# A feature-map attention with a squared-ReLU feed-forward: the last chunk's tiles of two batches each stored by one transfer

## The chip, the cores and the metric

The kernel runs on one core of a Trainium2 chip. A core has five engines with instruction queues of their own: TensorE (PE, matrix products; its weight loads are listed as PEld), VectorE (DVE), ScalarE (ACT), GpSimd (POOL) and SyncE (SP). SP does no arithmetic; here it issues transfers. ACT and POOL issue transfers too. The transfers themselves are carried by 16 DMA engines that all queues share. The metric is the device time of one execution in microseconds, lower is better.

## What is computed

Eight batches of 576 tokens with 8 heads of 64 values go through an attention with a feature map, and its output, 4608 tokens of 512 values, through two matrix products with a squared ReLU between them:

```python
def phi(x):
    proj = np.einsum('bhsd,df->bhsf', x, w_phi)
    proj = proj - np.max(np.abs(proj), axis=-1, keepdims=True)
    return np.concatenate([np.exp(proj), np.exp(-proj)], axis=-1)
q_p, k_p = (phi(q), phi(k))
kv = np.einsum('bhsf,bhsd->bhfd', k_p, v)
z = np.sum(k_p, axis=2)
num = np.einsum('bhsf,bhfd->bhsd', q_p, kv)
den = np.einsum('bhsf,bhf->bhs', q_p, z)[..., None] + 1e-06
attn = num / den                        # 8 x 8 x 576 x 64
x = attn.transpose(0, 2, 1, 3).reshape(4608, 512)
h = np.maximum(x @ w_in, 0.0)           # w_in 512 x 2048
out = h * h @ w_out                     # w_out 2048 x 512, out 4608 x 512 float32
```

## The kernel before

The feed-forward works in nine chunks of 512 tokens (`NCH = 9`). The chunks 0 to 7 hold the first 512 tokens of one batch each. The ninth, chunk 8, collects what is left: the last 64 tokens of all eight batches. It has four tiles of 128 tokens, `tt` = 0 to 3, and tile `tt` holds the tails of the batches `2*tt` (partitions 0 to 63) and `2*tt + 1` (partitions 64 to 127). In the output those two groups of 64 rows lie 576 rows apart.

For each chunk, `ffn_in` (line 745) makes the hidden layer on PE, `relu_sq` (line 721) applies ReLU and squares on ACT, DVE and POOL, and `ffn_out` (line 807) makes one tile of 128 tokens by 512 outputs per `tt` in PSUM (line 816), copies it on ACT or DVE into one of three float32 buffers `ot` (line 824), and stores it. In chunks 0 to 7 the store is one transfer of 128 rows on SP (line 835). In chunk 8 it is two transfers of 64 rows, one for each batch (line 832), both on SP except for tile 2, whose second half ACT issues.

The last tile of the program, chunk 8 and `tt` = 3, goes through `last_out` (line 772). There the 512 output columns are split into two halves of 256, with a PSUM bank each (line 780). Half 0 is copied by ACT (line 796), half 1 by DVE (line 794), into the buffer `otl`, and each half is stored by two transfers of 64 rows (line 803): batch 6 on SP, batch 7 on ACT. So half 0 and half 1 make four transfers.

All work is first recorded as operations by `add`, and then issued in the order of a table of numbers, `ORDER` (line 892); each engine runs its instructions in the order in which they are issued. `pin` ties each instruction to the one before it on its engine. An operation's instructions are those that its function `fn` issues when its turn comes. A transfer that is issued on SP or ACT waits at the head of that engine's queue until the copy it stores has been made. At the end of the program SP waits for all transfers to land, and then the engines meet and the program closes (recorded as line 1029).

Of the kernel before, what the change touches and what calls it, by code (L numbers as in the profile page):

```python
# [20 lines left out]
def act_cost(n):  # L21
    return max(n / 1200 + 0.050, 0.105), n / 1200 + 0.165 + SEM


def dve_cost(n):
    return n / 960 + 0.064, n / 960 + 0.150 + SEM
# [6 lines left out]
def pe_cost(n, each):  # L33
    return n * each, n * each + 0.165 + SEM
# [23 lines left out]
class Plan:  # L58
# [6 lines left out]
    def add(self, eng, cost, fn, r=(), w=(), opens=None, closes=None, dma=None, tiled=False, release=False, what=""):  # L65
        op = Op(eng, cost, fn, opens, closes, dma, tiled, release, len(self.ops), what)
        before = {}

        def after(o, wait):
            before[o] = max(before.get(o, 0.0), wait)  # L70

        for t in r:
            o = self.writer.get(t)
            if o is not None:
                after(o, 0.0 if o.eng == eng == "PE" else 1.0)
        for t in w:
            o = self.writer.get(t)
            if o is not None:
                after(o, 0.0 if o.eng == eng else 1.0)
            for o in self.readers.get(t, ()):  # L80
                after(o, 0.0 if o.eng == eng else 1.0)
        for t in r:
            self.readers.setdefault(t, []).append(op)
        for t in w:
            self.writer[t] = op
            self.readers[t] = []
        before.pop(op, None)
        for o, wait in before.items():
            o.succ[op] = wait
        op.n = len(before)  # L90
        self.ops.append(op)
        self.banks.extend(op.opens)
        return op
# [18 lines left out]
def kernel(  # L112
# [10 lines left out]
    nc = tc.nc  # L123

    B, H, S, D = q.shape
# [10 lines left out]
    def dep(i, before, kind):  # L136
        tc.add_manual_dep(i, before, mybir.DependencyInfo(kind, mybir.DependencyReason.DATA), reason="order")

    def pin(ins):
        i = ins.ins  # L140
        before = last_on.get(i.engine)
        if before is not None:
            dep(i, before, mybir.DependencyClass.NoSync)
        last_on[i.engine] = i.name
        if now[0].seq in GATES:
            dep(i, plan.ops[GATES[now[0].seq]].ins, mybir.DependencyClass.Sync)
        now[0].ins = i.name
        return ins
# [5 lines left out]
    def sb(name, shape, dt=BF16):  # L154
        return pool.tile([P, *shape], dt, name=name)

    def ring(name, n, shape, dt=BF16):
        return [sb(f"{name}{i}", shape, dt) for i in range(n)]
# [28 lines left out]
    ot = ring("ot", 3, [DM], F32)  # L187
    otl = sb("otl", [DM], F32)
# [4 lines left out]
    def copy(out, in_):  # L193

        if now[0].eng == "DVE":
            pin(nc.vector.tensor_copy(out=out, in_=in_))  # L196
        else:
            pin(nc.scalar.activation(out=out, in_=in_, func=ACT.Copy))
# [4 lines left out]
    def ps1(g):  # L203
        return psum[:, g.base, :]
# [564 lines left out]
    opb = {}  # L769
    oslot = [0]  # L770

    def last_out(c, tt, part):

        if part == 0:
            opb[c, tt] = [Bank(1, "op"), Bank(1, "op")]
        gs = opb[c, tt]
        def mm(half):
            def fn():
                for mc in range(4 * part, 4 * part + 4):
                    pin(nc.tensor.matmul(out=ps1(gs[half])[:, :256], lhsT=h2[c % 2][mc // 4][:, mc % 4, tt * P : (tt + 1) * P],  # L780
                                         rhs=wout[mc // 4][:, mc % 4, half * 256 : half * 256 + 256],
                                         start=(mc == 0), stop=(mc == MC - 1)))
            return fn
        for half in range(2):
            add("PE", pe_cost(4, 0.109), mm(half),
                r=[("wout", part)] + [("h2", c % 2, 4 * part + i, tt) for i in range(4)],
                w=[gs[half]], opens=gs[half] if part == 0 else None, what="F2h")
        if part < 3:
            return
        for half in range(2):  # L790
            def fn(half=half):
                o, i_ = otl[:, half * 256 : half * 256 + 256], ps1(gs[half])[:, :256]
                if half:
                    pin(nc.vector.tensor_copy(out=o, in_=i_))
                else:
                    pin(nc.scalar.activation(out=o, in_=i_, func=ACT.Copy))
            add("DVE" if half else "ACT", (dve_cost if half else act_cost)(256), fn, r=[gs[half]],
                w=[("otl", half)], closes=gs[half], what="oth")
        for half in range(2):
            for u, (name, e) in enumerate((("SP", nc.sync), ("ACT", nc.scalar))):  # L800
                def fn(half=half, u=u, e=e):
                    b = 2 * tt + u
                    pin(e.dma_start(out=out[b * S + 512 : b * S + 576, half * 256 : half * 256 + 256],
                                    in_=otl[u * 64 : u * 64 + 64, half * 256 : half * 256 + 256]))
                add(name, (0.5, 2.4), fn, r=[("otl", half)], what="stl")

    def ffn_out(c, tt, part):
        if (c, tt) == (NCH - 1, 3):
            last_out(c, tt, part)
            return  # L810
        if part == 0:
            opb[c, tt] = Bank(1, "op")
        g = opb[c, tt]
        def fn():
            for mc in range(4 * part, 4 * part + 4):
                pin(nc.tensor.matmul(out=ps1(g), lhsT=h2[c % 2][mc // 4][:, mc % 4, tt * P : (tt + 1) * P],  # L816
                                     rhs=wout[mc // 4][:, mc % 4, :], start=(mc == 0), stop=(mc == MC - 1)))
        add("PE", pe_cost(4, 0.216), fn, r=[("wout", part)] + [("h2", c % 2, 4 * part + i, tt) for i in range(4)],
            w=[g], opens=g if part == 0 else None, what="F2")
        if part == 3:  # L820
            sl = oslot[0] % 3
            oslot[0] += 1
            def fn():
                copy(ot[sl], ps1(g))
            o = add("ACT", act_cost(512), fn, r=[g], w=[("ot", sl)], closes=g, what="ot")
            plan.either((o, "DVE", dve_cost(512)))
            for u in range(2 if c == NCH - 1 else 1):
                def fn(u=u):
                    if c == NCH - 1:
                        b = 2 * tt + u  # L830
                        e = nc.scalar if tt == 2 and u else nc.sync
                        pin(e.dma_start(out=out[b * S + 512 : b * S + 576, :], in_=ot[sl][u * 64 : u * 64 + 64, :]))
                    else:
                        o = out[c * S : c * S + 512, :].rearrange("(p j) n -> j p n", j=4)[tt]
                        pin(nc.sync.dma_start(out=o, in_=ot[sl]))
                add("ACT" if c == NCH - 1 and tt == 2 and u else "SP", (0.5, 0), fn, r=[("ot", sl)], dma=(0.37 if c == NCH - 1 else 0.74, HW_IN, "st"), what="st")
# [22 lines left out]
    for c in range(NCH + 1):  # L859
        if c + 1 < B:  # L860
            b = c + 1
# [18 lines left out]
    for op in plan.arrange():  # L880
        if op.seq in FILL:
            now[0] = filler
            bank, n, col = FILL[op.seq]
# [150 lines left out]
```

## Time and profile before

| | us |
|---|---|
| median of three runs | 352.79 (352.58 to 352.99) |
| the profiled execution, whole | 352.66 |
| its span, from the first to the last instruction | 350.5 |
| PE busy | 338.9 |
| DVE busy | 273.2 |
| ACT busy | 228.4 |
| POOL busy | 96.8 |

The span is what the profile covers; the whole time of that execution is 2.2 us longer. The time of the runs is the whole time. The granted clock of PE was 1.000 over the span.

The profile is read from several views. The page gives busy times, a strip of 40 equal slices with the busy share in tenths, and the chain of waits that ended last. The same chain can be had in order of time. A view of instructions in order of time lists start and duration, with `SPq` and `ACTq` for a transfer's issue on that queue, which counts the issuing alone and not the transfer; consecutive instructions of one line are merged into one row with their count (x5). A view of the DMA packets gives, for a window, their number and bytes, by size, and for each queue the share that their durations make of 16 engines' time in the window. The queue of SP is q1 there, that of ACT is q10.

### The profile page before, as it was taken

How to read it: one execution, taken by the hardware profiler on the slowest of the kernel's cores; microseconds unless marked ns; L12 is line 12 of the kernel's file. 1: busy time of each engine (PE TensorE's matmuls, PEld its weight loads, DVE VectorE, ACT ScalarE, POOL GpSimd, SP SyncE). 2: the span in 40 equal slices, each digit the busy share in tenths (PEclk: the TensorE clock that was granted, in tenths of full speed). 3: DMA queues.
4: the chain of work that ended last, by engine and by line, in shares of the span. 5: the costliest groups of instructions: out<-in, count | busy, mean ns of one | idle time of the engine just before them, and what ended most of it. 6: DMA issues, size and time to landing. Idle time of an engine off the chain costs nothing.

```text
span 350.5 us, 8394 instructions
## 1 busy us (share of the span) xinstructions
PE 338.9 (97%) x3344; PEld 192.5 (55%) x3380; DVE 273.2 (78%) x521; ACT 228.4 (65%) x431; POOL 96.8 (28%) x144
## 2 busy tenths in 40 slices
PE   8889999999999999999999999999999999999995
PEld 5669976544654555455546554555545544444452
DVE  4999998899979988989877897999786932374332
ACT  4999897599779775787898569885954222321110
POOL 8735450397518510289104050000000000000000
PEclk9999999999999999999999999999999999999999
DMA  8999999899999997899957499792762610100114
GB/s 95 180 200 202 197 98 150 154 123 172 176 187 132 161 146 147 190 121 158 147 121 136 56 143 175 138 189 54 148 144 70 138 45 30 62 30 0 62 62 118
DMA packets 114917, 44.31 MB, mean 126 GB/s; under 512 B 83392, under 2 KB 110400, under 8 KB 114880
## 3 DMA queue, kind: packets, MB, share of 16 engines
q0 software_dynamic: 45216, 18.36, 46.7%
q1 hardware_dynamic: 69344, 25.14, 35.1%
q8 instruction: 26, 0.43, 0.5%
q10 hardware_dynamic: 320, 0.30, 0.2%
q14 instruction: 11, 0.09, 0.1%
HBM read 36.77 MB, written 9.44 MB: 132 GB/s over the span
## 4 chain that ended last, share of the span: by engine, by line
PE 78%; DVE 10%; ACT 7%; issue 3%; DMA 1%; DVEq 0%; ACTq 0%; POOLq 0%
PE psum L816 30%; PE psum L751 27%; PE psum L607 5%; PE psum L355 4%; PE psum L473 3%; PE psum L762 3%; DVE va L443 3%; ACT qf L592 2%; PE psum L577 2%; DVE mk L410 2%; DVE mq L517 2%; DVE h L735 2%; ACT kn L416 1%; PE psum L780 1%; DMA xk<-in_k_dram 1%
## 5 line engine op out<-in xcount | busy, mean ns | idle before, releaser
L816 PE MATMUL psum<-wout,h 128*128 128x512 bf16 x524 | 130.1, 379 | 2.2 <-issue 0.6
L751 PE MATMUL psum<-xT,win 128*128 128x512 bf16 x448 | 108.1, 379 | 0.3
L726 ACT ACTIVATE hr<-psum 128x512 bf16<-128x512 f32 x97 | 56.3, 596 | 68.8 <-PE psum L751 43.7
L816 PEld LDWEIGHTS <-h 128*128 128x128 bf16 x560 | 50.9, 98 | 55.4 <-issue 0.8
L751 PEld LDWEIGHTS <-win 128*128 128x128 bf16 x512 | 47.4, 98 | 54.0 <-issue 2.5
L735 DVE TENSOR_TENSOR h<-hr 128x512 bf16<-128x512 bf16 x143 | 55.9, 414 | 9.9 <-ACT hr L726 9.5
L592 ACT ACTIVATE qf<-psum 128x1024 bf16<-128x1024 f32 (+1 forms) x60 | 54.6, 942 | 10.7 <-PE psum L577 9.4
L517 DVE TENSOR_REDUCE mq<-psum 128x8 f32<-128x1024 f32 (+1 forms) x40 | 44.1, 1109 | 3.0 <-PE psum L355 2.1
L728 DVE TENSOR_SCALAR hr<-psum 128x512 bf16<-128x512 f32 x47 | 31.8, 685 | 17.7 <-PE psum L751 16.1
L410 DVE TENSOR_REDUCE mk<-psum 128x8 f32<-128x1024 f32 (+1 forms) x35 | 38.2, 1110 | 5.2 <-PE psum L355 5.2
L416 ACT ACTIVATE kp<-psum 128x1024 bf16<-128x1024 f32 (+1 forms) x35 | 32.7, 935 | 9.8 <-DVE mk L410 9.5
L607 PEld LDWEIGHTS <-qf 128*128 128x128 bf16 x640 | 28.3, 97 | 13.3 <-issue 1.1
L254 POOL DMA_DIRECT2D xv<-in_v_dram x26 | 19.3, 752 | 52.1 <-DVE va L443 41.5
L619 DVE TENSOR_TENSOR psum<-psum,en 128x520 f32<-128x520 f32 (+1 forms) x40 | 27.7, 699 | 7.4 <-PE psum L607 5.8
L416 ACT ACTIVATE kn<-psum 128x1024 bf16<-128x1024 f32 (+1 forms) x35 | 32.6, 935 | 0.0
L443 DVE TENSOR_TENSOR va<-xv,va 64x256 bf16<-64x256 bf16 (+2 forms) x68 | 30.4, 461 | 1.0 <-ACT va L435 0.3
L607 PE MATMUL psum<-kv,qf 128*128 128x65 bf16 x640 | 31.0, 193 | 0.0
L631 DVE TENSOR_TENSOR xo<-psum,rden 128x512 bf16<-128x512 f32 (+1 forms) x40 | 27.3, 685 | 0.8
L254 POOL DMA_DIRECT2D xk<-in_k_dram x28 | 20.8, 748 | 9.4 <-ACT va L429 5.1
L196 DVE COPY ot<-psum 128x512 f32<-128x512 f32 x16 | 10.8, 681 | 14.7 <-PE psum L816 13.4
L473 PE MATMUL psum<-va,kp 128*128 128x65 bf16 x256 | 19.5, 193 | 0.8 <-DVE va L443 0.4
L274 POOL DMA_DIRECT2D xq<-in_q_dram x24 | 17.6, 736 | 7.4 <-ACT kp L416 3.9
(68 smaller groups left out, 370.5 us busy)
## 6 DMA issues: line engine op xcount, KB each, us to landing
out_dram<-ot SPq DMA_DIRECT2D x32, 256.0 KB, 2.8
xk<-in_k_dram POOLq DMA_DIRECT2D x26, 128.0 KB, 4.4
xq<-in_q_dram POOLq DMA_DIRECT2D x24, 128.0 KB, 6.0
xv<-in_v_dram POOLq DMA_DIRECT2D x24, 128.0 KB, 4.7
win<-in_moe_w_in_dram POOLq DMA_DIRECT2D x4, 512.0 KB, 11.7
wout<-in_moe_w_out_dram POOLq DMA_DIRECT2D x4, 512.0 KB, 11.7
xq<-in_q_dram POOLq DMA_DIRECT2D x4, 256.0 KB, 6.5
xv<-in_v_dram POOLq DMA_DIRECT2D x2, 512.0 KB, 9.3
```

Of the source, the lines that this page charges most:

```text
L254: pin(nc.gpsimd.dma_start(out=x[:, a * 512 : z * 512].rearrange("p (h x) -> p h x", x=4 * D), in_=src[b][2 * a : 2 * z, 0:512, :].rearrang ...
L410: pin(nc.vector.tensor_reduce(out=mk_view(g), in_=ps2(pj)[:, :, : n * Fd].rearrange("p e (i f) -> p e i f", f=Fd), axis=AX.X, op=ALU.max, ...
L416: pin(nc.scalar.activation(out=dst[slot][:, :, :n, :].rearrange("p e i f -> p e (i f)"), in_=ps2(pj)[:, :, : n * Fd], func=ACT.Exp, scale= ...
L443: pin(engine().tensor_tensor(out=t[:, :, :D].rearrange("p m (x c) -> p m x c", c=2), in0=x.rearrange("p (m x c) -> p m x c", m=n, c=2), in ...
L517: pin(nc.vector.tensor_reduce(out=mqb[:, c, :, :n], in_=ps2(pj)[:, :, : n * Fd].rearrange("p e (i f) -> p e i f", f=Fd), axis=AX.X, op=ALU ...
L592: pin(nc.scalar.activation(out=o, in_=i_, func=ACT.Exp, scale=sgn))
L607: pin(nc.tensor.matmul(out=o[:, u // 4, u % 4 * D1 : (u % 4 + 1) * D1], lhsT=(qp, qn)[sg][slot][:, u * m : u * m + P], rhs=kv_sb[s2][:, h ...
L726: pin(nc.scalar.activation(out=hr[sl], in_=ps1(g), func=ACT.Relu))
L728: pin(nc.vector.tensor_scalar(out=hr[sl], in0=ps1(g), scalar1=0.0, scalar2=None, op0=ALU.max))
L735: pin(engine().tensor_tensor(out=dst, in0=i_, in1=i_, op=ALU.mult))
L751: pin(nc.tensor.matmul(out=o, lhsT=win[mc // 4][:, kc, mc % 4 * P : (mc % 4 + 1) * P], rhs=x, start=(kc == 0), stop=(kc == KC - 1)))
L816: pin(nc.tensor.matmul(out=ps1(g), lhsT=h2[c % 2][mc // 4][:, mc % 4, tt * P : (tt + 1) * P], rhs=wout[mc // 4][:, mc % 4, :], start=(mc = ...
```

## The change

A helper `rest(tt)` views the output as batch, row, column and takes the rows 512 to 575 of the two batches of tile `tt`: a target of 2 x 64 x (columns). Line 832's two transfers become one on SP, with that target and the whole 128-partition buffer as its source. In `last_out` each half tile becomes one transfer with the same kind of target: half 0 on SP, half 1 on ACT. The operations and the table `ORDER` stay; an operation whose transfer is gone issues nothing.

```diff
+    def rest(tt):
+        return out.rearrange("(b s) n -> b s n", s=S)[2 * tt : 2 * tt + 2, 512:576, :]
+
     def last_out(c, tt, part):
 
         if part == 0:
...
         for half in range(2):
             for u, (name, e) in enumerate((("SP", nc.sync), ("ACT", nc.scalar))):
                 def fn(half=half, u=u, e=e):
-                    b = 2 * tt + u
-                    pin(e.dma_start(out=out[b * S + 512 : b * S + 576, half * 256 : half * 256 + 256],
-                                    in_=otl[u * 64 : u * 64 + 64, half * 256 : half * 256 + 256]))
+                    if u == half:
+                        pin(e.dma_start(out=rest(tt)[:, :, half * 256 : half * 256 + 256],
+                                        in_=otl[:, half * 256 : half * 256 + 256]))
                 add(name, (0.5, 2.4), fn, r=[("otl", half)], what="stl")
...
             for u in range(2 if c == NCH - 1 else 1):
                 def fn(u=u):
                     if c == NCH - 1:
-                        b = 2 * tt + u
-                        e = nc.scalar if tt == 2 and u else nc.sync
-                        pin(e.dma_start(out=out[b * S + 512 : b * S + 576, :], in_=ot[sl][u * 64 : u * 64 + 64, :]))
+                        if u == 0:
+                            pin(nc.sync.dma_start(out=rest(tt), in_=ot[sl]))
```

The end of SP's queue before, from the last store of an earlier chunk (line 835) on. Each row is one transfer, target, source and the target's shape; `ot_140` to `ot_142` are the three buffers `ot`:

```order
L835 DMA out_dram<-ot_140 128x512
L803 DMA out_dram<-otl 64x256
L832 DMA out_dram<-ot_142 64x512
L832 DMA out_dram<-ot_141 64x512
L832 DMA out_dram<-ot_142 64x512
L832 DMA out_dram<-ot_140 64x512 x2
L803 DMA out_dram<-otl 64x256
```

and with the change, where the same lines have the numbers 837, 806 and 834:

```order
L837 DMA out_dram<-ot_140 128x512
L806 DMA out_dram<-otl 2x64x256
L834 DMA out_dram<-ot_142 2x64x512
L834 DMA out_dram<-ot_141 2x64x512
L834 DMA out_dram<-ot_140 2x64x512
```

Seven issues behind the 128-row store have become four, the queue now ends with the tile of `ot_140`, and the targets lead with 2 where they led with 64.

The end of ACT's queue before:

```order
L198 ACTIVATE ot_140<-psum 128x512
L796 ACTIVATE otl<-psum 128x256
L198 ACTIVATE ot_141<-psum 128x512
L803 DMA out_dram<-otl 64x256
L832 DMA out_dram<-ot_141 64x512
L803 DMA out_dram<-otl 64x256
```

and with the change:

```order
L198 ACTIVATE ot_140<-psum 128x512
L799 ACTIVATE otl<-psum 128x256
L198 ACTIVATE ot_141<-psum 128x512
L806 DMA out_dram<-otl 2x64x256
```

ACT keeps one transfer of three, half 1 of `otl` with both batches, behind the same copies as before.

## The prediction, made before the changed kernel ran

> **What bounds the kernel now.** I read the page first, then the chain of waits in order of time for the last 10 us, then the instructions in order of time there, and last the DMA packets in short windows. The page says who sets the length of the whole:
>
> ```profile
> span 350.5 us, 8394 instructions
> PE 338.9 (97%) x3344; PEld 192.5 (55%) x3380; DVE 273.2 (78%) x521; ACT 228.4 (65%) x431; POOL 96.8 (28%) x144
> DMA  8999999899999997899957499792762610100114
> PE 78%; DVE 10%; ACT 7%; issue 3%; DMA 1%; DVEq 0%; ACTq 0%; POOLq 0%
> ```
>
> PE is busy for 338.9 of 350.5 us, and 78% of the chain that ended last lies on it. The DMA engines are the opposite: in most of the last ten slices (8.8 us each) their mean busy share is a tenth or two at most. A change of stores that touches no matmul can therefore act only where PE has nothing left to do, and that is the end. The chain of waits in order of time closes so:
>
> ```profile
> 340.74 4.48 PE psum L816 x20
> 345.22 1.32 PE psum L780 x12
> 346.55 0.02 issue
> 346.57 0.42 DVE otl L794
> ```
>
> PE's last matmul ends at 346.55, DVE copies the last half tile until 346.99 (346.57 + 0.42), and from there to 350.5 no compute runs at all: 3.5 us in which only the last stores travel and the program closes. These are the instructions in order of time, DMA issues among them (columns: start, us, engine, line, operation):
>
> ```profile
> 340.49 0.53 SPq L803 DMA_DIRECT2D out_dram<-otl  x1
> ...
> 343.39 3.75 SPq L832 DMA_DIRECT2D out_dram<-ot  x5
> ...
> 343.59 0.51 ACTq L803 DMA_DIRECT2D out_dram<-otl  x1
> 344.20 0.58 ACTq L832 DMA_DIRECT2D out_dram<-ot  x1
> ...
> 346.57 0.42 DVE L794 COPY otl<-psum 128x256 f32<-128x256 f32 x1 [0.56 <-PE psum L780]
> 347.03 0.47 ACTq L803 DMA_DIRECT2D out_dram<-otl  x1
> 347.23 0.55 SPq L803 DMA_DIRECT2D out_dram<-otl  x1
> ```
>
> The copy releases two stores: ACT's half goes at once, at 347.03, while SP's is held to 347.23, because SP still issues the stores of line 832 until 347.14 (343.39 + 3.75). These ten issues, seven on SP and three on ACT, are the whole of what the diff edits. The individual starts on SP that I need come from two shorter windows of the same view, one around each:
>
> ```profile
> 344.15 1.10 SPq L832 DMA_DIRECT2D out_dram<-ot  x2
> ```
>
> ```profile
> 346.03 0.47 SPq L832 DMA_DIRECT2D out_dram<-ot  x1
> ```
>
> So the tile of ot_142 is issued from 343.39, that of ot_141 from 344.15, that of ot_140 from 346.03.
>
> **How a store is spread now.** The price of the change depends on the DMA engines, so here are the packets. First a 128-row store of an earlier chunk, the only one in the window from 338.0 to 339.4 us:
>
> ```profile
> DMA packets 144, 0.26 MB, mean 187 GB/s; under 512 B 16, under 2 KB 16, under 8 KB 144
> q1 hardware_dynamic: 144, 0.26, 49.9%
> ```
>
> Next, one 64-row half of the last tile, from 341.3 to 342.4 us (its first row is the busy share in 40 slices of 0.0275 us):
>
> ```profile
> DMA  0000000000000661994995595231100000000000
> DMA packets 80, 0.07 MB, mean 60 GB/s; under 512 B 16, under 2 KB 80, under 8 KB 80
> q1 hardware_dynamic: 80, 0.07, 26.4%
> ```
>
> A store of 128 rows makes 128 + 16 packets, one of 64 rows 64 + 16: one packet for each row of the target, and sixteen small ones, one for each DMA engine that took part. Both numbers of rows divide evenly by 16, so each engine carries 8 rows or 4. The busy share gives the price of a row on its engine: 49.9% of 1.4 us on 16 engines is 11.18 us, and 11.18 / 128 = 87 ns for 2 KB (the sixteen small ones stay in, so this is a little high). In the second window 26.4% of 1.1 us on 16 is 4.65 us, over 64: 73 ns for 1 KB. Among the last packets both kinds differ (346.9 to 348.4 us in slices of 0.0375, then 348.35 to 349 in slices of 0.01625):
>
> ```profile
> DMA  0000001939494579957890339893979099288992
> DMA packets 144, 0.25 MB, mean 169 GB/s; under 512 B 20, under 2 KB 20, under 8 KB 144
> q1 hardware_dynamic: 144, 0.25, 78.2%
> ```
>
> ```profile
> DMA  0062691193893999979979939799515423020000
> q1 hardware_dynamic: 101, 0.08, 38.3%
> q10 hardware_dynamic: 80, 0.07, 29.7%
> ```
>
> The first of these holds the two stores of ot_140: 78.2% of 1.5 us on 16 is 18.77 us for 124 rows, 151 ns for 2 KB. In the second, ACT's half (queue q10) takes 29.7% of 0.65 us on 16, 3.09 us, over 64: 48 ns for 1 KB. So a row has cost from 87 to 151 ns, a half row from 48 to 73. From issue to first packet it is 341.66 - 340.49 = 1.2 us for the half tile and 347.13 - 346.03 = 1.1 us for ot_140; the last packet of the program ends at 348.94 (36 slices), and 1.6 us later the span is over.
>
> **The change, part by part.** It takes away four issues: two on SP (the second halves of ot_142 and ot_140 fold into the first, ot_141's second half moves from ACT's queue into SP's transfer, and SP no longer takes half 1 of otl) and two on ACT. No compute instruction moves, and nothing waits for these stores but the end of the program, since no later tile needs their buffers. What it saves is small: the last issue goes from 347.23 to 347.03, 0.2 us at most. ACT's two issues at 343.59 and 344.20 stood behind its last real work, so they are worth nothing.
>
> What it adds is the shape. All five new stores name their target as 2 x 64 rows, because two batches' tails are not adjacent in the output; the order of instructions above shows 2x64x512 and 2x64x256 where 64x512 and 64x256 stood. If a transfer is shared out among engines by the leading count of its target, as the even shares of 64 and 128 rows suggest, then a leading count of 2 yields two shares of 64 rows and fourteen engines stand idle. I take this as the forecast, with all five transfers on the same two engines, one behind the other, since nothing in the trace shows a transfer that starts its shares elsewhere. The sum goes by 87.3 and 48 ns, the lower rows: eight rows in a queue on one engine went at 87 ns in the store at 338 us, and I expect two engines to be in each other's way less than sixteen, not more:
>
> half 0 of otl: first packet 341.66, 64 x 0.048 = 3.07, done at 344.73. ot_142, issued 343.39, could begin 1.1 later at 344.49, and so begins at 344.73; ot_141 (344.15 + 1.1) and ot_140 (346.03 + 1.1) are ready before their turn comes. Three times 64 x 0.0873 = 5.59 is 16.76: 361.49. Half 1 of otl, in between or at the end, adds 3.07: 364.56. With the 1.6 us that follow the last packet the span is 366.2 instead of 350.5, longer by 15.7. The profiled execution took 352.66, so 368.3; the median of the runs shown is 352.79, 0.13 above it, which changes nothing.
>
> Bounds: with 151 ns and 73 ns for all packets, half 0 ends at 341.66 + 4.67 = 346.33, three tiles take 28.99 and half 1 4.67, end 379.99 + 1.6 = 381.6, which is 31.1 more: 383.8. Below: the second KB of a row costs 87.3 - 48 = 39 ns, so if rows of a long queue cost by their bytes alone, 2 KB take 79 ns; ot_142 from 344.49, 192 x 0.0786 = 15.09, half 1 of otl wholly in the gaps that the tiles leave, end 359.58 + 1.6 = 361.2, 10.7 more: 363.3. The value stays near the lower end, since it was measured on rows in a queue with one store in flight.
>
> The Trainium skill speaks on both sides here, on its page "DMA: Bandwidth & Descriptors". In the section "Why a DMA increments its semaphore by 16 and not by 1" it says that the number of engines is the largest one up to 16 that divides the slowest dimension of both access patterns, and that these are the lowest-numbered ones; that is two engines here, the same two for all five stores. The sixteen completion packets of 64 and 128 rows agree with it, and no run here shows a smaller count. In "Rules for kernel authors" the same page advises one 128-partition transfer in place of two halves, which by itself would give the first rival's time.
>
> **The rivals.** First, *not slower*: the shares are cut by the tile's 128 rows, and sixteen engines carry 8 each. Then ot_140 leaves in one piece, 347.13 + 8 x 0.0873 = 347.83, in place of two halves that last to 348.4; half 1 of otl can begin 1.1 after its issue, at 348.13, and ends 8 x 0.048 = 0.38 later, at 348.51 against 348.94: 352.2. With 73 ns it ends at 348.38 (where its first packet came in the row above) + 0.58 = 348.96, no gain: 352.7. For it: 128 rows on the tile's side, and the 128-row store at 338 us that ran so. Against it: that store led with 128 on both sides. It decides as long as at least eight engines carry the rows: with eight, ot_140 ends at 347.13 + 1.40 = 348.53, half 1 at 349.30, 0.4 us more (353.0); with four, the three tiles queue from 344.49 to 352.87, half 1 ends at 354.41, and the time is 358.2.
>
> Second, *two engines each, but not the same two*: the transfers run beside each other. The last tile ends at 347.13 + 5.59 = 352.72, half 1 sooner, at 348.38 + 3.07 = 351.45; with 1.6 us the span is 354.3, 3.8 more: 356.5. Against it: no row shows that engines are taken in turn.
>
> **How the numbers follow.** The forecast has 0.80: every even share in the trace follows a leading count, and the new one is 2. The sixteen-engine rival has 0.14, of which 0.02 for a gain over 0.2% (0.7 us, about what a measurement of this kernel can tell from no change), since its own bounds end at 0.5 us of gain; the separate pairs, with the case of four engines, 0.06. Faster 0.02, within 0.2% 0.12, slower 0.86. The range holds the forecast with its bounds, 363.3 to 383.8, and leaves the rivals' 0.20 out.
>
> **What would show it.** Right: 130 packets, not 144, for one tile's store; from about 344.5 us the busy share of the DMA engines at an eighth; landings of the three tiles that grow one after the other by about 5.5 us (now the longest takes 2.6, below); PE's last matmul still at 346.5; and some 18 us of pure DMA behind it. If landings stay below 3 us, the sixteen-engine rival was right; if they are all near 7 us and alike, the separate pairs. If the tiles land 9 us apart, the mechanism holds and my price for a row was too low. Anything that moves before 340 us would be outside all of this.
>
> ```profile
> DMA to landing us min/median/max: 2.2/2.4/2.6
> ```
>
> (line 832's six issues today.)

## The result, and the profile after

| | before | with the change |
|---|---|---|
| median of the runs, us | 352.89 (4 runs, 352.58 to 353.14) | 367.96 (4 runs, 367.49 to 368.26) |
| span of the profiled execution, us | 350.5 | 365.7 |
| PE busy, us | 338.9 | 338.1 |

The change makes the kernel slower, by a factor of 1.0423 (95% interval 1.0392 to 1.0455). The prediction said 368.3 us. The granted clock of PE reads 0.977 over the longer span; it is 1.00 in each stretch up to 346.6 us and 0.56 behind it, where PE has nothing left to do, so it slowed no matmul. The page of the changed kernel begins like this:

```profile
span 365.7 us, 8386 instructions
PE 338.1 (92%) x3344; PEld 192.1 (53%) x3380; DVE 273.2 (75%) x521; ACT 228.8 (63%) x431; POOL 96.8 (26%) x144
PE   7889999999999999999999999999999999999900
DMA  8999989899989996899664999628544002001111
```

The engines do the same work. New is an end of two slices (9.1 us each) in which PE does nothing at all, and in which the DMA engines show a share of one tenth, not nine. That is the sign to look for: the end lasts long although most of the DMA engines have nothing to do.

In order of time, the instructions of the end (the same columns as in the prediction) move by 0.05 us up to the last copy, and then the issues differ:

```profile
340.54 0.69 SPq L806 DMA_DIRECT2D out_dram<-otl  x1
...
343.44 4.79 SPq L834 DMA_DIRECT2D out_dram<-ot  x3
...
346.62 0.42 DVE L797 COPY otl<-psum 128x256 f32<-128x256 f32 x1 [0.56 <-PE psum L783]
347.08 1.13 ACTq L806 DMA_DIRECT2D out_dram<-otl  x1
```

What SP waits for after that, from the view of SP's own waits between 347 and 366 us (who, for whom: us in total, times, longest):

```profile
SPq L1031 <- DMA out_dram<-ot: 16.1, 1, 16.1
```

The program's last line waits 16.1 us for the store of a tile; before, its waits for stores were 1.1 us together. The packets say why. From 344.9 to 364.1 us, the time of the three tiles and of half 1:

```profile
DMA  1111011111111111111111111111111111111111
DMA packets 528, 0.92 MB, mean 48 GB/s; under 512 B 10, under 2 KB 144, under 8 KB 528
q1 hardware_dynamic: 398, 0.79, 11.2%
q10 hardware_dynamic: 130, 0.13, 1.9%
```

ACT's queue, q10, carries one store there, half 1 of `otl`, with 128 + 2 packets, where a 128-row store of the kernel before had 128 + 16. Two engines took part. The two shares together, 13.1%, are just over the 12.5% that two engines of sixteen can give (the recorded times of neighbouring packets overlap a little). The price of a row: 11.2% of 19.2 us on 16 engines is 34.4 us, over 384 rows, 90 ns for 2 KB (the last few packets of half 0 stay in); half rows 1.9% of the same over 128, 46 ns. In the middle of it, from 350.8 to 358.7 us, both queues move the same number of packets:

```profile
q1 hardware_dynamic: 131, 0.26, 8.6%
q10 hardware_dynamic: 130, 0.13, 4.7%
```

A row of a tile and a half row of half 1 take turns on each of the two engines. Half 1 is issued last of all and is done 5 us before the last tile: the end belongs to `ot_140`, the last on SP's queue. From 361 to 364.5 us, in slices of 0.0875 us, it ends at 361 + 34 x 0.0875 = 364.0:

```profile
DMA  1111111111111111111111111111111111000000
q1 hardware_dynamic: 77, 0.15, 11.3%
```

The price of a row is not the same all the way. While the first tile is under way, from 345.6 to 346.6 us, and near the end, from 361 to 362, the queue shows

```profile
q1 hardware_dynamic: 13, 0.03, 12.5%
```

```profile
q1 hardware_dynamic: 26, 0.05, 13.7%
```

which is 12.5% of 16 us over 13 rows, 154 ns, and then 13.7% over 26, 84 ns.

### The profile page after: what moved, and what is told of

It is laid out like the page before. It is cut to its first block, busy times and chain, and to the rows that moved or that the text cites. A ratio compares the mean times of both kernels' runs of the same rounds, so it can differ in the third digit from the quotient of the medians.

```text
span 365.7 us, 8386 instructions
## 1 busy us (share of the span) xinstructions
PE 338.1 (92%) x3344; PEld 192.1 (53%) x3380; DVE 273.2 (75%) x521; ACT 228.8 (63%) x431; POOL 96.8 (26%) x144
## 4 chain that ended last, share of the span: by engine, by line
PE 74%; DVE 12%; ACT 4%; issue 3%; DMA 2%; POOL 0%; DVEq 0%; ACTq 0%; POOLq 0%
PE psum L819 29%; PE psum L751 26%; PE psum L607 5%; PE psum L355 4%; PE psum L473 3%; PE psum L762 3%; DVE va L443 3%; DVE mq L517 2%; PE psum L577 2%; DVE mk L410 2%; DMA xq<-in_q_dram 2%; DVE h L735 1%; ACT qf L592 1%; DVE mk L389 1%; ACT kn L416 1%
## 5 line engine op out<-in xcount | busy, mean ns | idle before, releaser
L592 ACT ACTIVATE qf<-psum 128x1024 bf16<-128x1024 f32 (+1 forms) x60 | 54.6, 937 | 11.2 <-PE psum L577 9.9
L728 DVE TENSOR_SCALAR hr<-psum 128x512 bf16<-128x512 f32 x47 | 31.9, 685 | 17.7 <-PE psum L751 16.1
```

The source lines that it names most:

```text
L592: pin(nc.scalar.activation(out=o, in_=i_, func=ACT.Exp, scale=sgn))
L728: pin(nc.vector.tensor_scalar(out=hr[sl], in0=ps1(g), scalar1=0.0, scalar2=None, op0=ALU.max))
```

## Experiments

Three theories stood against each other. **A**: a transfer gets as many engines as the leading count of its target allows, and always the same ones. **B**: a target of two levels is slow in itself. **C**: each transfer has engines of its own, or the serial order is that of a queue.

The kernel before ran again beside each group of these; its medians lie from 352.62 to 352.89, and a ratio is to the runs beside it. The interval of a ratio reaches 0.1 to 0.3% to either side, which is 0.3 to 1.1 us.

| run | median, us | ratio to the kernel before (95% interval) |
|---|---|---|
| the change: 2 leads | 367.96 | 1.0423 (1.0392 to 1.0455) |
| 4 leads | 360.04 | 1.0199 (1.0183 to 1.0215) |
| 8 leads | 354.45 | 1.0042 (1.0026 to 1.0057) |
| 64 leads | 352.69 | 0.9998 (0.9984 to 1.0013) |
| 2 leads, one tile on ACT's queue | 367.82 | 1.0428 (1.0410 to 1.0446) |
| only the three tiles changed | 365.13 | 1.0352 (1.0329 to 1.0375) |
| only the half tiles changed | 355.36 | 1.0062 (1.0042 to 1.0082) |
| PE reads alternately, 64 leads | 369.88 | 1.0486 (1.0469 to 1.0503) |
| DVE writes alternately, 64 leads | 352.91 | 1.0004 (0.9995 to 1.0012) |
| before, one more 64-row store issued by ACT | 352.80 | 1.0002 (0.9989 to 1.0016) |
| 8 leads, tiles issued by ACT | 355.43 | 1.0075 (1.0060 to 1.0089) |

**The leading count alone.** Three kernels change nothing but the helper `rest`, which says where a tile's rows go; queue, number of transfers and bytes stay. A tile's rows then land in other rows of the output than they should, so these kernels serve to time the stores and nothing else.

```diff
     def rest(tt):
-        return out.rearrange("(b s) n -> b s n", s=S)[2 * tt : 2 * tt + 2, 512:576, :]
+        return out.rearrange("(b s) n -> b s n", s=S)[2 * tt : 2 * tt + 2, 512:576, :].rearrange("b s n -> s b n")
```

> The changed kernel with the two levels of each of the five targets exchanged: 64 rows lead and the 2 batches come second (64x2x512, 64x2x256). It is still one transfer for 128 partitions, the same queue, the same bytes; rows of the two batches are stored in another order, so the output's rows are permuted. Theory A (a transfer uses as many engines as its target's leading count allows, always the same ones): sixteen engines again, 144 packets for a tile, time 352.2 to 352.8 us, as the first rival of the prediction had it. Rival B (a target of two levels is slow in itself, whichever leads): 368 us as with the change.

```diff
+        return out.rearrange("(b s) n -> b s n", s=S)[:, 512 + tt * 16 : 528 + tt * 16, :]
```

> The changed kernel with targets that lead with 8: each tile goes to 16 rows of every one of the 8 batches (8x16x512, 8x16x256); the output's rows are permuted. Theory A: eight engines with 16 rows each, 16 x 84 ns = 1.35 us for a tile, so no tile waits for the one before; last packet 0.3 us later than before the change, 352.9 to 353.2 us, and 136 packets for a tile. Rival B: 368.

```diff
+        return out.rearrange("(b s) n -> b s n", s=S)[tt // 2 * 4 : tt // 2 * 4 + 4, 512 + tt % 2 * 32 : 544 + tt % 2 * 32, :]
```

> The changed kernel with targets that lead with 4: each tile goes to 32 rows of 4 batches (4x32x512, 4x32x256); the output's rows are permuted. Theory A: four engines with 32 rows each at 84 ns, 2.7 us for a tile; three tiles and half 1 queue from 344.5 to 344.5 + 3 x 2.7 + 1.5 = 354.1, with 1.5 us behind the last packet the span is 355.6 and the time 357.8. Rival B: 368.

With 64 in the lead the two-level target costs nothing that can be measured: 352.69, ratio 0.9998 (0.9984 to 1.0013). This is the same transfer as the change's in all but the order of its two levels, so B falls. From 348.4 to 349.1 us of that kernel, half 1 of `otl`:

```profile
DMA  0000001819659699899993998966763221000000
q10 hardware_dynamic: 144, 0.13, 55.1%
```

144 packets, sixteen engines. With 4 in the lead, from 344.5 to 356.2 us:

```profile
DMA  1504002312222222222222222231222222222210
q1 hardware_dynamic: 396, 0.79, 21.3%
q10 hardware_dynamic: 132, 0.13, 3.2%
```

132 packets for half 1 and a share of two to three tenths: four engines. With 8 in the lead, from 344.8 to 350.5 us:

```profile
q1 hardware_dynamic: 408, 0.79, 44.9%
```

408 packets are 384 rows and 3 x 8: eight engines. The counts are exactly those of A. The times are not: 354.45 where 352.9 to 353.2 was expected, 360.04 where it was 357.8. With 8 in the lead a row cost 44.9% of 5.7 us on 16, 40.9 us over 384, 107 ns in place of 84 (the row near the end of the changed kernel, above). On each engine 48 rows at 23 ns more are 1.1 us, most of what the run lay above its expectation. With 4 in the lead it is 21.3% of 11.7 us on 16 over 384, 104 ns; 96 rows at 20 ns more are 1.9 of the 2.2 us. The extra cost is not spread evenly; two windows of 1 us of the same kernel, 345 to 346 and 346.5 to 347.5:

```profile
DMA packets 26, 0.05 MB, mean 53 GB/s; under 512 B 0, under 2 KB 0, under 8 KB 26
q1 hardware_dynamic: 26, 0.05, 45.6%
```

```profile
DMA packets 102, 0.19 MB, mean 195 GB/s; under 512 B 7, under 2 KB 7, under 8 KB 102
q1 hardware_dynamic: 102, 0.19, 53.2%
```

While the first tile begins, a packet lasts 45.6% of 16 us over 26, 281 ns; later 53.2% over 95 rows, 90 ns. So the first tile begins haltingly, as in the changed kernel, and the rows behind it run at 84 to 90 ns. With 64 in the lead nothing of the kind shows: 56.7% of 3.7 us on 16 from 344.7 to 348.4 us is 87 ns for all 384 rows. Whether that is a matter of SP's queue was tried with one more kernel:

```diff
-                            pin(nc.sync.dma_start(out=rest(tt), in_=ot[sl]))
+                            pin(nc.scalar.dma_start(out=rest(tt), in_=ot[sl]))
```

> The kernel with 8 in the lead, with one edit: ACT issues the three tiles in place of SP. With SP a row cost 105 ns on its engine (384 rows on eight engines from 344.9 to 350.2 us) and the time was 354.45. If the queue of SP is what makes rows dear, as the 64-row stores suggest (146 ns from SP beside 84 ns from ACT in the kernel before), a row costs 84 to 88 ns from ACT, the three tiles end 0.8 to 1.0 us sooner and the time is 353.5. If eight engines make it dear, whoever issues: 105 ns and 354.4.

It was 355.43, slower by another microsecond, and the rows are no cheaper (344.8 to 352.2 us, 7.4 us: 42.0% on 16 is 49.7 us, for 379 rows in that window and 128 half rows at 46 ns, so 116 ns a row; the GB/s are in 40 slices of 0.185 us):

```profile
GB/s 100 55 33 33 44 44 155 177 177 221 177 133 100 100 66 100 111 122 166 144 177 233 166 155 155 199 216 177 188 221 166 161 161 111 78 61 22 0 0 0
DMA packets 539, 0.91 MB, mean 123 GB/s; under 512 B 32, under 2 KB 160, under 8 KB 539
q10 hardware_dynamic: 539, 0.91, 42.0%
```

From 345.0 to 345.9 us the stores move only 33 to 55 GB/s, and they halt once more about 347.5. So the halting start isn't SP's. What causes it stays open. On ACT the issue did harm of another kind: the first one held ACT's own next copy back, to 344.71 from 343.58 in the changed kernel.

```profile
343.42 1.19 ACTq L834 DMA_DIRECT2D out_dram<-ot  x1
344.71 0.60 ACT L198 ACTIVATE ot<-psum 128x512 f32<-128x512 f32 x1 [4.22 <-issue]
```

**The same engines, or others.** One tile of the changed kernel goes to the other queue.

```diff
-                            pin(nc.sync.dma_start(out=rest(tt), in_=ot[sl]))
+                            pin((nc.scalar if tt == 2 else nc.sync).dma_start(out=rest(tt), in_=ot[sl]))
```

> The changed kernel with one edit: the tile of ot_141 (tile 2 of the last chunk) is issued by ACT in place of SP, with the same 2x64x512 target. Theory A: the same two engines carry all five transfers whoever issues them, so the time stays, 367.5 to 368.5 us, and the packets of the two queues alternate. Rival C (the serial order is that of SP's queue, and a transfer on another queue finds other engines or other time): SP's two tiles take 345.0 + 2 x 5.4 = 355.8, ACT's ends sooner, the span is 357.3 and the time 359.5.

367.82, as with the change. Two queues share the work (344.8 to 363.9 us), and nothing is gained, because both feed the same two engines: their shares together are 13.1%, no more than the two engines of the change.

```profile
q1 hardware_dynamic: 267, 0.53, 7.6%
q10 hardware_dynamic: 260, 0.39, 5.5%
```

C falls: neither the queue's order nor a free choice of engines sets the time.

**One part at a time.** Each kernel keeps the other part of the change as it was before (line 803's four transfers of 64 rows in the first, line 832's six in the second).

> Only the three tiles have the new store (2x64x512 on SP); the last half tiles go out in four transfers of 64 rows as before. Theory A: the three tiles queue on two engines, 3 x 64 rows x 84 ns = 16.1 us from 344.5, and the half rows of half 1 that fall to these engines add 8 x 46 ns = 0.4: last packet 361.0, span 362.5, time 364.7. If each transfer had two engines of its own: 347.1 + 5.4 = 352.5 and 356.2 us.

> Only the last half tiles have the new store (2x64x256, half 0 on SP and half 1 on ACT); the three tiles go out in six transfers of 64 rows as before. Theory A: half 1 begins 1.3 us after its issue at 347.05 and takes 64 x 46 ns = 2.9 us on each of two engines: last packet 351.3, span 352.8, time 355.0. If the tiles alone were the cause: 352.7.

365.13 and 355.36, each 0.4 us above its expectation. Taken alone the parts cost 365.13 - 352.87 = 12.3 and 2.5 us, together 14.8, against 15.1 for the change. The half tile's cost is plain to see (350.1 to 353.6 us, where its 130 packets are nearly all that moves). The execution that was profiled took 357.01 us, 1.65 above the median; its last copy begins at 348.33 in place of 346.57, so all its times here are 1.8 us late:

```profile
DMA  4210202001111111111011111111111111111100
q10 hardware_dynamic: 130, 0.13, 11.9%
```

Where only the tiles are changed, SP's last two issues, the third tile's and half 1's, show how far two engines fall behind:

```profile
345.55 2.88 SPq L834 DMA_DIRECT2D out_dram<-ot  x1
348.53 4.70 SPq L806 DMA_DIRECT2D out_dram<-otl  x1
```

They keep SP for 2.88 and 4.70 us; in the kernel before an issue there took 0.47 to 0.59.

**One transfer with the output in order.** If the rows of a tile alternate between the two batches, 64 can lead and the output is in order. Two places for the alternation were tried, each on top of the kernel with 64 in the lead. PE, where it reads the last chunk's tokens:

```diff
                 x = xS[:, :, kc, :] if c == NCH - 1 else xT[c % NXT][kc // 2][:, :, kc % 2, :]
+                if c == NCH - 1:
+                    x = x.rearrange("p t (b s) -> p t s b", b=2)
+                    o = ps1(g).rearrange("m (t s b) -> m t s b", s=64, b=2)
```

> A version that computes the reference with one transfer for each tile and 64 rows in the lead: in the last chunk PE reads the tokens of the two batches alternately (the moving tile xS as 64 tokens x 2 batches), so the row of a tile is 2 x token + batch and the target is 64x2x512. Theory A: sixteen engines, 352.2 to 352.8 us if PE reads every 64th pair of values as quickly as neighbours; its 64 matmuls for the last chunk take 14 us, and if the strided reading halved their speed, 14 us more. Rival B (two levels are slow in themselves): 368.

369.88. The groups of that line, from the view of one line (minimum, median and maximum of a duration in ns):

```profile
L754 PE MATMUL psum<-xT,win x448: 376/379/391, 71.4 to 312.8; 128*128 128x512 bf16 x150
L754 PE MATMUL psum<-xS,win x64: 642/644/646, 301.2 to 350.6; 128*128 128x512 bf16 x64
```

A matmul that reads values 128 bytes apart takes 644 ns in place of 379; 64 x 0.265 = 17.0 us, and the run is 17.3 us above the kernel before. The durations of neighbouring matmuls overlap, so the time that PE is busy with these 64 says it better: it goes from 15.3 us in the kernel before to 32.4. The Trainium skill says on its page "SBUF — State Buffer", in the section "Door 1: The DMA port swizzle (why `[64,N]` ≈ `[32,N]`)", that each access to a new line of 16 bytes pays a penalty; this run agrees.

Then DVE, where it writes the squares of the last chunk:

```diff
+            if c == NCH - 1:
+                pin(engine().tensor_tensor(out=dst.rearrange("p (t s b) -> p t b s", s=64, b=2),
+                                           in0=i_.rearrange("p (t b s) -> p t b s", b=2, s=64),
+                                           in1=i_.rearrange("p (t b s) -> p t b s", b=2, s=64), op=ALU.mult))
+                return
```

> Another version that computes the reference with one transfer for each tile and 64 rows in the lead: the tokens of the two batches are brought into alternation by DVE, where it writes the square of the last chunk's hidden layer (16 of its 143 squares, each to every second place of 2 bytes); PE reads as before, 379 ns a matmul. Theory A: sixteen engines, the time of the kernel with 64 rows in the lead, 352.5 to 352.9. If a square that writes every second place takes as long as a copy to 4-byte values (688 in place of 418 ns), DVE has room for 16 x 0.27 us, but the last square stands 0.1 us before the matmuls that need it and PE may wait some tenths: up to 353.5.

352.91, ratio 1.0004 (0.9995 to 1.0012). The 16 squares are dearer, at 724 ns in place of 418, but DVE has the room:

```profile
L736 DVE TENSOR_TENSOR h<-hr x16: 712/724/737, 310.7 to 336.4; 128x512 bf16<-128x512 bf16 x16
```

This is what the change was to be: one transfer for each tile, the output in order, at the price of no measurable time. It gains none either.

**The issue on SP.** In the kernel before, SP's part of the last store waits 0.2 us for the issues of `ot_140`. One of these goes to ACT.

```diff
-                        e = nc.scalar if tt == 2 and u else nc.sync
+                        e = nc.scalar if tt and u else nc.sync
```

> The kernel before with one edit: the second half of ot_140 (tile 1 of the last chunk) is issued by ACT in place of SP, as tile 2's already is. SP is then free at 346.5 and issues its part of the last half tile at 347.03 in place of 347.23; both halves of ot_140 travel at once. Expected: 0.2 to 0.4 us less than before, 352.4 to 352.7. If the last packets are bound by the DMA engines alone and not by the issue, no change, 352.8 to 352.9.

352.80, ratio 1.0002, though both last issues now start together, as soon as the copy is done:

```profile
347.16 0.47 SPq L803 DMA_DIRECT2D out_dram<-otl  x1
347.16 0.50 ACTq L803 DMA_DIRECT2D out_dram<-otl  x1
```

The interval, 0.9989 to 1.0016, would hide a gain of 0.2 us, but the trace would not: SP's issue now stands 0.46 us behind the start of the last copy (346.70), where it stood 0.66 behind it, and the last packets end as far behind that start as before, 2.4 us (at 349.08; before, at 348.94 with the copy at 346.57). So the 0.2 us of issue was not what the end waited for. No version was measurably faster than the kernel before.

## Why the prediction was right, point by point

- **What bounds the end.** Right: PE, the copies and the issues up to the last copy moved by 0.05 us, and the whole loss lies behind it.
- **What the change takes away.** Miscounted: five issues go, three on SP and two on ACT, where the prediction says four. No term of its sum rests on the count.
- **Two engines, the same two.** Right, and shown from three sides: 130 packets; the time follows the leading count 2, 4, 8, 64 with the rest held; a second queue gains nothing. The rule of the Trainium skill that the prediction cited (page "DMA: Bandwidth & Descriptors", section "Why a DMA increments its semaphore by 16 and not by 1") agrees with all four counts.
- **The sum.** It put the last packet at 364.56, which came at 364.0; a row at 87.3 ns, which was 90; a half row at 48, which was 46; 1.6 us behind the last packet, which were 365.7 - 364.0 = 1.7. The terms were each off by a few per cent, and in both directions, so that the sum came this close is in part luck: past the first tile the rows went faster than forecast, one in 80 ns on each engine at the end (75 rows on two engines in 3.0 us), which over 192 rows is 1.4 us less, and the halting rows of the first tile gave much of it back.
- **The lower rows of the price.** Right to choose, for the average: two engines were in each other's way no more than sixteen. A price like the 151 ns of the upper bound came back only in the first tile, 154 ns for about a microsecond.
- **First rival, sixteen engines.** Its price was 352.2 to 352.7; the kernel with 64 in the lead makes it true and takes 352.69. The gain of 0.4 us that its lower end saw does not show in the time, for one reason that the trace gives: half 1 is issued at 347.22 in that kernel and its first packet comes at 348.4 + 6 x 0.0175 = 348.5, 1.3 us later. The prediction had 1.1, from SP's store, though ACT's half took as long in its own row (348.38 - 347.03). It began no sooner for the tile being done sooner.
- **Eight and four engines.** 353.0 and 358.2 were forecast, 354.45 and 360.04 measured. The mechanism held and the size was off: rows were priced as if each store ran at full speed from its first packet, and they cost 107 and 104 ns.
- **Second rival, engines of its own for each transfer.** Refuted, 356.5 forecast.
- **Signs.** The packets and the DMA share came as announced. Landing times, from which the order of the tiles was to be read, are not in the view for these stores: it gives none for a transfer on fewer than sixteen engines here. The packets had to serve.

## What to carry to other kernels

Before two stores are folded into one, look at the leading count of the new target: one that leads with 2 puts 128 rows on two engines, and the last stores of a program have nothing to hide behind. Where the count can't be kept, keep the two transfers; folding them saved nothing measurable here even with sixteen engines. If a stretch ends late while the DMA share stands at a constant small tenth, count the small packets of a store: here there was one for each engine that took part.

## What the runs showed of the hardware that was not expected

- The rows of the first tile halt where a store uses fewer engines: 281 ns a packet from 345 to 346 us with eight engines, 90 later. In the kernel before, the two 64-row stores of `ot_140` from SP cost 151 ns a row too, though on sixteen engines. The cause of both is open.
- An issue can keep its queue long: 4.70 us for one store on SP while the two engines were behind, where 0.5 is usual. On ACT it delays compute: 1.19 us with eight engines. There no packet of an earlier store was still moving (none from 342.95 to 344.7 us), so why that issue was long is open.
- Two queues that feed the same engines share them evenly by packets, 131 to 130, though one's rows are twice as large, so the store that was issued last was not the one that ended last. It began late, too: half 1 was issued at 347.08, and its packets lie between 350.8 and 358.7 us, while its first one in the kernel before came 1.35 us after the issue.
